# Rows of experts 1 to 7 gathered whole, sorted in DRAM and loaded again in the layout of the transposes; the last batch's routing in fewer steps

## The chip, the core and the metric

The kernel runs on one core of a Trainium2 chip. The metric is the device time of one execution in microseconds. TensorE (PE) does the products, VectorE (DVE) and ScalarE (ACT) the elementwise work, GpSimd (POOL) issues the gathers and scatters (indirect DMAs), and SyncE (SP) issues all other DMAs from one queue, in its program order.

## The reference

Attention over 4 batches, 8 heads, 768 positions and 64 columns a head, with 4 sink positions and a window of 128; then a mixture of 8 experts with two chosen for each of the 3072 tokens.

```python
x = attn_out.transpose(0, 2, 1, 3).reshape(B * S, H * D)          # 3072 x 512
noisy_logits = x @ w_gate + np.log1p(np.exp(x @ w_noise)) * noise
top2 = np.argpartition(-noisy_logits, 2, axis=1)[:, :2]
...                                                               # softmax over the two: top2_w
for e in range(E):
    for k in range(2):
        mask = top2[:, k] == e
        h = np.maximum(x[mask] @ w1[e], 0.0)                      # 512 -> 1024
        out[mask] += top2_w[mask, k, None] * (h @ w2[e])          # 1024 -> 512
```

## The kernel before

Phase one (to about 181 us) is the attention. It leaves each token's row in a DRAM array `x_rows`: 544 floats, in four quarters of 136 (`SW`: 128 columns of x and the 8 gate weights of the token). Phase two routes the last batch and runs the experts. Experts are sorted by their count of tokens; the first in that order is "expert 0" here, and capacities are 832 rows for the first four and 768 for the others, so an expert has 7 tiles of up to 128 rows or 6.

All work is recorded as operations of a planner, `Plan` (L80), each with an engine, a planned duration, a priority and the data that it reads and writes. Its `run` places them by a simulation of its own and writes a fixed program for every engine. So the order on each engine, and on SP's queue, is set by the planned durations, the priorities and the number of buffers; at run time an engine only waits for semaphores. `Plan.dma` records the issue on SP and the transfer.

**Expert 0** takes 4 tiles from batches 0 to 2 and 3 tiles (4 to 6) after the last batch is routed. Its rows are gathered whole (`go` in `gather`, L995, 128 rows of 544 floats), turned on PE (`rows_turn`, L1066), split into a high and a low half (ACT L1075, DVE L305), multiplied with w1 (`up`, L1285 to 1287), passed through ReLU (`up_h` on ACT, L1299; `up_l` on DVE, L1306) and multiplied with w2 (`down`, L1317 to 1323).

**Experts 1 to 7** form the first product by a scheme of seven half-size products (`seven`, L1420 to 1422). It needs x transposed, which DVE does in 32x32 blocks (`rows_seven`, L1194); for a tile to come out transposed in whole, each partition must hold four rows' quarters in a certain order. Therefore a tile is gathered in four pieces by quarters (`part`, L1001: 128 pieces of 136 floats), by an index table `rt_idq` with one entry for each quarter, which `spread` (PE L935, four groups of matmuls, DVE L938) builds at the end of the last batch's routing. There are 174 such gathers. They go into four buffers `xg`. After the transposes come the splits and sums of the scheme (DVE L305, ACT L1208). Weights are loaded by SP in pieces of 512 KB into two buffers `st` (`w_chunk`, L1102), and split by ACT (L1111, L1152) and DVE (L305, L1160). Before a tile's gathers stands a copy on POOL (`begun`, L1012) that holds them until the expert before has come to a certain point. The second product is L1451 and L1454; ends of a tile are ACT L1326 or ACT L1329 and DVE L1333, L1337, and the scatter that adds into the output is POOL L1341. The zeros of the output are written by SP (L1608).

**Routing of the last batch** runs while PE works on expert 0: logits (PE L710, DVE L721, L726), the top two (DVE L803, L807), the one-hot table `m` (L816), the ranks by matmuls with it (PE L824 to 830), one-hot tables of position and of tile (DVE L878 to 885), the place of each token in the experts' lists (PE L895), the order of the experts (`ordered`, DVE L955 to 967), the indices `idg` (L919) of expert 0's tiles 4 to 6, and `rt_idq`.

Of the kernel before, what the change touches and what calls it, by code (L numbers as in the profile page):

```python
# [9 lines left out]
F32 = mybir.dt.float32  # L10
# [65 lines left out]
PORT = 9  # L76
# [554 lines left out]
def routing_setup(nc, pool, tmp, cst, sh):  # L631
# [14 lines left out]
    iota("io", [128, 128], [[1, 128]], 0, 0)  # L646
    iota("io1", [128, E * TE], [[1, E * TE]], 1, 0)
# [48 lines left out]
def logits(nc, plan, cst, sh, b, jj, z):  # L696
# [4 lines left out]
    xa, li = plan.next("X"), b * (NT // 2) + jj  # L701
    last = b == sh.B - 1
    tk, mk = ("lt", li), ("lm", li)
# [3 lines left out]
    def proj():  # L707
        p = get("X", xa, [128, 4, 128], F32, "ps")
        for i, g in enumerate(pairs):
            nc.tensor.matmul(p[32 * i:32 * (i + 1), :2, :], c["wbd"][:, i].rearrange("p h a e -> p (h a e)"),  # L710
                             get("xtn", g, [128, sh.S])[:, jj * 256:(jj + 1) * 256], start=True, stop=True)

    def copy():
        nc.scalar.activation(get(*tk, [128, 2, 128], F32, "sb"), get("X", xa)[:, :2, :], AF.Copy)

    def turn():
        for i in range(2):
            nc.tensor.transpose(get("X", xa)[:, 2 + i, :], get(*tk)[:, i, :], c["idf"])

    def scale():  # L720
        nc.vector.tensor_tensor(get(*mk, [128, 2, H, 2 * E], F32, "sb"),  # L721
                                get("X", xa)[:, 2:, :].rearrange("p t (h e) -> p t h e", h=H),
# [7 lines left out]
    op("PE", .57, z, proj, r=[("xt", n) for n in ns] + [("rc", 0)], w=[("X", xa)], u=[("xtn", g) for g in pairs] + region)  # L730
    op("ACT", .27, z, copy, r=[("X", xa)], w=[tk], u=region)
    op("PE", .25, z, turn, r=[tk], w=[("X", xa)], u=region)
    op("DVE", .34, z, scale, r=[("X", xa)] + [("rin", n // 2) for n in ns], w=[mk], u=[("ri", b)] + region)
# [3 lines left out]
def routing(nc, plan, cst, sh, b, t0, nt, z, xbuf):  # L737
# [31 lines left out]
    def step(eng, dur, fn, r=(), w=(), u=(), kind=0):  # L769
        u = [*u, ("old", 0)] if last else u  # L770
        plan.op(eng, dur, z if last else plan.now + PR.get("rt", .5), fn, [t(x) if isinstance(x, str) else x for x in r],
                [t(x) if isinstance(x, str) else x for x in w], u, kind=kind)

    def dve(fn, r, w, dur=.07 + .001 * 8 * nt, u=(), kind=0):
        step("DVE", dur, fn, r, w, u, kind)
# [4 lines left out]
    side = "DVE" if last else "Pool"  # L780
    s_ = v if last else gp

    def aux(fn, r, w, cols=8):
        step(side, .07 + .001 * cols * nt if last else .15 + .0021 * cols * nt, fn, r, w, kind=PORT)
# [36 lines left out]
    def rank():  # L821
# [12 lines left out]
    aux(lambda: s_.tensor_tensor(rt("z")[:, 1], rt("mx")[:, :, 1], rt("mx")[:, :, 0], op=OP.subtract), ["mx"], ["z"], 1)  # L834
    act(lambda: nc.scalar.activation(rt("z")[:, 1], rt("z")[:, 1], AF.Exp), [], ["z"])
    aux(lambda: s_.tensor_scalar(rt("den", [128, nt]), rt("z")[:, 1], 1.0, 1e-9, op0=OP.add, op1=OP.add), ["z"], ["den"], 1)
    dve(lambda: v.reciprocal(rt("z")[:, 0], rt("den")), ["den"], ["z"], .1)
    aux(lambda: s_.tensor_tensor(rt("z")[:, 1], rt("z")[:, 1], rt("z")[:, 0], op=OP.mult), [], ["z"], 1)
    aux(lambda: s_.tensor_tensor(rt("wd", full), rt("oh"), rt("z")[:, :, :, None].to_broadcast(full), op=OP.mult),
        ["oh", "z"], ["wd"], 16)  # L840
    aux(lambda: s_.tensor_tensor(rt("w", ab_), rt("wd")[:, 0], rt("wd")[:, 1], op=OP.add), ["wd"], ["w"])
# [16 lines left out]
    if last:  # L858
# [4 lines left out]
        dve(lambda: v.tensor_scalar(rt("v0", n0), c["slot"][:, 0, sh.FA:], rt("cnt")[:, :1], None, op0=OP.is_lt), ["cnt"], ["v0"], .07)  # L863
        dve(lambda: v.tensor_scalar(rt("e0", n0), rt("v0"), -1.0, 1.0, op0=OP.mult, op1=OP.add), ["v0"], ["e0"], .07)
        dve(lambda: v.tensor_scalar(rt("e0"), rt("e0"), c["dum"], 128.0, op0=OP.mult, op1=OP.add), [], ["e0"], .07)
# [5 lines left out]
    dve(lambda: v.tensor_scalar(rt("pp", pair, I32), rt("g"), 127, None, op0=OP.bitwise_and), ["g"], ["pp"], .08)  # L871
    dve(lambda: v.tensor_scalar(rt("tq", pair, I32), rt("g"), 7, None, op0=OP.logical_shift_right), ["g"], ["tq"], .08)
    dve(lambda: v.tensor_scalar(rt("vl", pair), rt("r2"), float(sh.CAP), None, op0=OP.is_lt), ["r2"], ["vl"], .08)
    dve(lambda: v.scalar_tensor_tensor(rt("tv", pair), rt("tq"), 1.0, rt("vl"), op0=OP.add, op1=OP.mult), ["tq", "vl"],
        ["tv"], .08)
    wide = [128, nt, E * TE]
    for k in range(2):
# [8 lines left out]
            [], [f"tc{k}"], 56)  # L886
    if not last:
        yield 1
# [24 lines left out]
    if last:  # L913
# [17 lines left out]
        quarters = lambda: get("X", xs, [128, 4, E * TE], F32, "ps", [128, 4, 128])  # L931

        def spread():
# [3 lines left out]
        step("PE", .5, spread, [("y", -3), "idw"], [("X", xs)])  # L937
        dve(lambda: v.scalar_tensor_tensor(get("rt_idq", b, [128, 4, E * TE], I32)[:, :, rest], quarters()[:, :, rest], 4.0,  # L938
# [829 lines left out]
```

## Time and profile before

| | us |
|---|---|
| median of 3 runs (761.93 to 764.37) | 762.06 |
| the profiled execution, its own time | 758.4 |
| its span | 756.7 |
| PE busy in the span | 704.2 (93%) |
| DVE busy | 548.9 (73%) |
| POOL busy | 432.0 (57%) |
| ACT busy | 410.0 (54%) |

All durations below are of the profiled execution. Its span leaves 1.7 us of its time outside, and its time is 3.66 us under the median. A row of the waits names the engine and line that waited, what ended the wait, and the total, the count and the longest in microseconds; "issue" is time in which the engine waited for nothing that the profile shows, and "remote" a release whose source it doesn't place. In the rows of stretches, PEclk is the granted clock of TensorE as a share of full speed and DMA the mean busy share of the 16 DMA engines.

### The profile page before, as it was taken

The numbers are of one execution on the slowest core, as the hardware profiler recorded it, in microseconds if no ns is written. First come the engines' busy times: TensorE is split into PE (matmuls) and PEld (weight loads), VectorE is DVE, ScalarE is ACT, GpSimd is POOL, SyncE is SP. The second block draws the span as 40 slices with busy tenths as digits, with TensorE's granted clock in tenths as the row PEclk, the third lists the DMA queues.
The fourth block names the chain that finished last, engine by engine and source line by source line (L and its number), as shares of the span: only waits on it lengthen the run. The fifth ranks groups of instructions, "written<-read, shape, count | busy, mean of one in ns | idle before, by whom it ended". The sixth has DMA issues, their size and how long they took to land.

```text
span 756.7 us, 13528 instructions
## 1 busy us (share of the span) xinstructions
PE 704.2 (93%) x4737; PEld 588.2 (78%) x4737; DVE 548.9 (73%) x1289; ACT 410.0 (54%) x924; POOL 432.0 (57%) x560
## 2 busy tenths in 40 slices
PE   5999998998998959999999999998999999899995
PEld 3665766666776949888988998797899889889984
DVE  6799999985734777785887688576958868595720
ACT  3978788784113455555564656454645655455521
POOL 5668798793075735575557565666746556651022
PEclk9999999999999979999999999999999999999998
DMA  8656787556252581438235632744472383454233
GB/s 295 175 180 192 218 248 185 188 124 197 72 186 46 93 228 44 138 76 161 65 114 94 144 97 78 129 111 135 89 161 68 115 172 94 127 99 105 56 43 43
DMA packets 59048, 98.08 MB, mean 130 GB/s; under 512 B 19264, under 2 KB 32576, under 8 KB 58976
## 3 DMA queue, kind: packets, MB, share of 16 engines
q1 hardware_dynamic: 45616, 69.99, 30.2%
q0 software_dynamic: 13360, 27.19, 20.9%
q8 instruction: 38, 0.62, 0.4%
q14 instruction: 34, 0.28, 0.1%
HBM read 68.95 MB, written 28.20 MB: 128 GB/s over the span
## 4 chain that ended last, share of the span: by engine, by line
PE 61%; DVE 13%; ACT 8%; DMA 7%; issue 5%; POOL 4%; SPq 0%; another core or an unknown queue 0%; POOLq 0%; DVEq 0%; ACTq 0%
PE Y L1451 19%; PE H L1420 5%; PE H L1422 5%; PE H L1421 5%; DMA out<-tmp,idx 3%; PE X L1420 2%; PE X L1421 2%; PE X L1422 2%; PE S L401 2%; POOL xg L1001 2%; ACT strip L522 2%; DMA st<-in_w2c 1%; DMA xg<-x_rows,idg 1%; DVE cbuf L412 1%; PE P L464 1%
## 5 line engine op out<-in xcount | busy, mean ns | idle before, releaser
L1001 POOL DMA_INDIRECT xg<-x_rows,rt_idq x174 | 183.4, 1054 | 60.2 <-issue 44.5
L1451 PE MATMUL Y<-w2a,hb 128*128 128x512 f32 x504 | 128.1, 393 | 0.0
L1451 PE MATMUL Y<-w2b,hb 128*128 128x512 f32 x504 | 125.6, 393 | 0.0
L1451 PEld LDWEIGHTS Y<-w2b,hb 128*128 128x128 f32 x504 | 94.5, 188 | 20.1
L1341 POOL DMA_INDIRECT out<-tmp,idx x34 | 62.9, 1849 | 81.8 <-ACT tmp L1326 68.5
L1451 PEld LDWEIGHTS Y<-w2a,hb 128*128 128x128 f32 x504 | 94.4, 188 | 19.0
L1421 PE MATMUL H<-x,wr 128*128 128x384 f32 (+1 forms) x224 | 77.9, 348 | 1.0 <-DVE x L305 1.0
L1420 PE MATMUL H<-xe,wr 128*128 128x384 f32 (+1 forms) x168 | 59.1, 352 | 13.9 <-ACT xe L1208 7.8
L305 DVE TENSOR_TENSOR wr<-st,wr 128x512 fp32r<-128x512 f32 (+1 forms) x86 | 60.0, 697 | 9.6 <-ACT wr L1152 8.8
L1152 ACT ACTIVATE wr<-st 128x512 fp32r<-128x512 f32 x84 | 52.3, 625 | 20.1 <-DVE st L305 19.8
L305 POOL TENSOR_TENSOR cbuf<-cbuf,mn 128x528 f32<-128x528 f32 x48 | 52.6, 1098 | 12.4 <-DVE mn L422 8.7
L1422 PE MATMUL H<-xe,wr 128*128 128x384 f32 (+1 forms) x168 | 58.3, 347 | 0.0
L401 PE MATMUL S<-kq 64*64 64x196 f32 (+1 forms) x768 | 47.8, 352 | 7.9 <-DVE cbuf L412 4.8
L1326 ACT ACTIVATE tmp<-Y,wc 128x512 f32<-128x512 f32 x31 | 21.3, 688 | 49.7 <-PE Y L1451 27.5
L1420 PEld LDWEIGHTS H<-xe,wr 128*128 128x128 f32 x168 | 31.9, 190 | 19.6 <-ACT xe L1208 8.2
L1341 POOL DMA_INDIRECT out<-turned,idx x18 | 31.7, 1758 | 25.6 <-ACT turned L1326 19.2
L1435 ACT ACTIVATE tmp<-H 128x384 f32<-128x384 f32 (+1 forms) x56 | 28.0, 500 | 32.8 <-PE H L1422 26.4
L1421 PEld LDWEIGHTS H<-x,wr 128*128 128x128 f32 x224 | 42.5, 190 | 3.1 <-DVE x L305 1.6
L1012 POOL COPY spacer<-hb 1x1 f32<-1x1 f32 x28 | 6.4, 230 | 66.0 <-ACT hb L1441 41.4
L412 DVE COPY_PREDICATED cbuf<-le,S 128x256 f32<-128x256 uint8 x80 | 33.7, 441 | 11.4 <-ACT cbuf L405 11.0
L401 PEld LDWEIGHTS S<-kq 64*64 64x64 f32 x768 | 22.5, 138 | 23.8 <-DVE cbuf L412 12.4
L1420 PE MATMUL X<-x,wr 128*128 128x384 f32 (+1 forms) x112 | 38.8, 347 | 0.4 <-DVE tmp L1438 0.4
(329 smaller groups left out, 1804.1 us busy)
## 6 DMA issues: line engine op xcount, KB each, us to landing
st<-in_w1c SPq DMA_DIRECT2D x32, 512.0 KB
st<-in_w2c SPq DMA_DIRECT2D x32, 512.0 KB
kq<-in_qk_t SPq DMA_DIRECT2D x15, 780.0 KB
out<-zt SPq DMA_DIRECT2D x31, 256.0 KB
vn<-in_v SPq DMA_DIRECT2D x16, 384.0 KB
x_rows<-strip SPq DMA_DIRECT2D x48, 128.0 KB
xg<-x_rows,rt_idq POOLq DMA_INDIRECT x174
st<-in_vsink SPq DMA_DIRECT2D x4, 512.0 KB
```

Source lines behind the costliest of these rows:

```text
L305: eng.tensor_tensor(out, a, b, op=OP.subtract)
L401: nc.tensor.matmul(whole[x, h, c0:c1], kq(g)[r, KS + 128 * j + 64 * s:KS + 128 * j + 64 * s + 64], kq(g)[r, o + c0:o + c1], start=True, st ...
L412: nc.vector.copy_predicated(c, le[:, None, :].to_broadcast([128, 2, 128]), p)
L1001: nc.gpsimd.indirect_dma_start(out=x[:, i, :], out_offset=None, in_=xbuf.rearrange("r (q d) -> (r q) d", d=sh.SW), in_offset=bass.Indirect ...
L1152: plan.op("ACT", .03 + .255 * m, z, lambda: nc.scalar.activation(h(), src(), AF.Copy), r=[st], w=[(*key, b)] + old, u=[key, ex], lat=P2["s ...
L1326: nc.scalar.activation(get("y", Y[e, t], [128, DM]), get("Y", Y[e, t]), AF.Copy, scale=c["wc"][e % 2][:, t:t + 1])
L1341: d = nc.gpsimd.indirect_dma_start(out=out, out_offset=bass.IndirectOffsetOnAxis(ap=c["idx"][:size(e, t), e, t:t + 1], axis=0), in_=get("y ...
L1420: nc.tensor.matmul(p, wh, h, start=start and not k, stop=False, skip_group_check=True)
L1421: nc.tensor.matmul(p, wh, l, start=False, stop=False, skip_group_check=True)
L1422: nc.tensor.matmul(p, wl, h, start=False, stop=k == 1, skip_group_check=True)
L1435: nc.scalar.activation(u_of(e, k), src(), AF.Copy)
L1451: nc.tensor.matmul(p, h[:, x * (CAP + R) + 128 * t:x * (CAP + R) + 128 * t + 128], w[:, y], start=(f == 0 and x + y == 0), stop=(f == FC - ...
```

## The change

**Rows.** For experts 1 to 7 a tile's rows are gathered whole, by one indirect DMA of 128 rows of 544 floats instead of four by quarters (45 gathers instead of 174), into one of two staging buffers `sg`. SP stores the tile into a DRAM array `x_sorted`, by quarters, and loads it again into one of two buffers `xg` so that each partition holds four consecutive rows of one quarter, which is the layout for the transposes. Each of the 45 tiles so adds a store and a load of 278 KB (the last tile of a 832-row expert loads half) to SP's queue. Expert 0's tiles go to `sg` and `xg` too, by the table `row_tile`. The copies that hold gathers back are moved: expert 1 has none; expert 2 waits for points in expert 0's second part; experts 3 to 7 for points two experts earlier.

**Routing of the last batch.** The index table needs one matmul and one cast (`rt_idi`) instead of four groups of matmuls and one larger DVE operation. The odd piece of the logits gets a PSUM buffer of its own (`TX`). The one-hot tables are written by 24 tensor-scalar operations, one a tile, instead of six tensor-tensor operations; the gate weights' operations go from DVE to POOL; some operations that nothing waits for soon come later (`after=9`).

**Expert 0.** `up` is recorded as four operations instead of one. Two splits of weights (128x1024 each, one of w1 and one of w2) go from DVE to POOL, and the last piece of w2 is loaded later.

```diff
+def row_tile(sh, e, t):
+    n = sh.first[e] + t
+    if e:
+        return "xg", n - sh.first[1] + 2
+    return ("xg", t - 2) if t in (2, 3) else ("sg", t - 2 * (t > 3))
...
-    for i in range(min(128, sh.CAPS[e] - 128 * t) // 32):
-        plan.op("Pool", P2["gather"], z + i, lambda i=i: part(i), r=[("rt_idq", sh.B - 1)] + held,
-                w=[("xg", n, i)], u=[("xg", n)], lat=(P2["rest"], P2["lands"]))
+    def store():
+        nc.sync.dma_start(rows.rearrange("q p d -> p q d"), stage().rearrange("p (q d) -> p q d", d=sh.SW))
+
+    def load():
+        x = plan.get(*row, [128, sh.XW], F32, "early")[:, :size // 32 * sh.SW]
+        nc.sync.dma_start(x, rows.rearrange("q (s i) d -> (q s) (i d)", i=4)[:, :size // 32 * sh.SW])
...
+    plan.op("Pool", P2["gather"], zs, sort, r=[("rt_idi", sh.B - 1)] + held, w=[sg], lat=P2["lands"])
+    plan.dma(zs, store, 1.6, r=[sg], w=[("xs", n)], late=P2["late"])
+    plan.dma(z, load, 1.4, r=[("xs", n)], w=[row], late=2)
...
-            for q in range(4):
-                nc.tensor.matmul(quarters()[:, q, rest], get("y", -3, [128, 4, 128])[:, q, :], idw()[:, rest], start=True, stop=True)
+        step("PE", .15, lambda: nc.tensor.matmul(spread()[:, rest], get("y", -3, [128, 128]), idw()[:, rest], start=True, stop=True),
+             [("y", -3), "idw"], [("X", xs)])
...
+    for k in range(2) if last else ():
+        dve(lambda k=k: rows_of(k), ["pp"], [f"op{k}"], .1 * nt, kind=PORT)
+        dve(lambda k=k: cols_of(k), ["tv"], [f"tc{k}"], .085 * nt, kind=PORT)
...
-            w_chunk(plan, nc, c, sh, w1, w2, 0, 1, 3, -60)
-            for i in (2, 3):
-                w_chunk(plan, nc, c, sh, w1, w2, 0, 2, i, -50)
+            w_chunk(plan, nc, c, sh, w1, w2, 0, 1, 3, -60, "Pool")
+            w_chunk(plan, nc, c, sh, w1, w2, 0, 2, 2, -50, "Pool")
...
-        if t < XG and e == 1:
-            k = 5 * t // 3
+        if e == 1:
+            return None
+        if e == 2:
+            k = FC + t
             return ("hh", k), lambda: hs(k)[:1, :1].bitcast(F32), ("h", k)
-        if t < XG:
-            return ("h", e - 1, 2 * t, 0, 0), lambda: mine(plan)[:1, 2 * t, :1].bitcast(F32), ("hb", e - 1)
-        n, i = sh.first[e] + t - 1, 3
-        return ("xg", n, i), lambda: get("xg", n).rearrange("p (i d) -> p i d", d=sh.SW)[:1, i, :1], ("xg", n)
+        return ("h", e - 2, t, 0, 0), lambda: mine(plan)[:1, t, :1].bitcast(F32), ("hb", e - 2)
...
-            {"st": 2, "w1": 4, "w2a": 2, "xg": XG, "wc": 2, "xe": 1, "wr": 1, "x7": 1},
+            {"st": 2, "w1": 4, "w2a": 2, "xg": 2, "sg": 2, "wc": 2, "xe": 1, "wr": 1, "x7": 1},
```

POOL from expert 0's tiles 4 to 6 (`idg`) through the first gathers of expert 1 (`rt_idq`, now `rt_idi`) to the first scatters (L1341, now L1374). Before:

```order
L995 DMA xg<-x_rows,idg 128x544 x3
L1012 COPY spacer<-hb 1x1
L1001 DMA xg<-x_rows,rt_idq 128x136 x16
L1340 MEMSET spacer 1x1
L1341 DMA out<-turned,idx 3968x512
L1012 COPY spacer<-xg 1x1
L1340 MEMSET spacer 1x1
L1341 DMA out<-tmp,idx 3968x512
L1001 DMA xg<-x_rows,rt_idq 128x136 x4
```

After:

```order
L1015 DMA sg<-x_rows,idg 128x544 x3
L1030 DMA sg<-x_rows,rt_idi 128x544 x5
L1045 COPY spacer<-hb 1x1
L1373 MEMSET spacer 1x1
L1374 DMA out<-turned,idx 3968x512
L1030 DMA sg<-x_rows,rt_idi 128x544
L1045 COPY spacer<-hb 1x1
L1373 MEMSET spacer 1x1
L1374 DMA out<-tmp,idx 3968x512
L1373 MEMSET spacer 1x1
L1374 DMA out<-tmp,idx 3968x512
L1030 DMA sg<-x_rows,rt_idi 128x544
```

Sixteen gathers of quarters (four tiles) become five whole gathers (five tiles) ahead of the first scatter; expert 1's tile 5 stands behind that scatter, and its tile 6 behind the third of them as listed.

SP's queue over the same time, with the semaphores that a row waits for (DMASW is a gather or scatter that has landed, DMAHW a transfer of SP's own). Before, between the last loads of the experts' numbers and the next weight load:

```order
L1608 DMA out<-zt 128x512 [waits DMAHW3_49]
L1608 DMA out<-zt 128x512 [waits DMAHW4_49]
L1608 DMA out<-zt 128x512 [waits DMAHW5_49]
L1102 ISA
L1102 DMA st<-in_w2c 128x1024 [waits DMAHW1_49,DMAHW6_49,DVE_49,Activation_49]
L1608 DMA out<-zt 128x512 [waits DMASW7_49,DMASW6_49,DMAHW7_49,DMASW5_49,DMASW0_49]
```

After, the store and the load of expert 1's last tile, up to the next weight load:

```order
L1035 DMA x_sorted<-sg 128x4x136 [waits DMAHW2_49,DMASW0_49]
L1642 DMA out<-zt 128x512 [waits DMASW6_49,DMASW7_49,DMASW4_49,DMASW1_49]
L1642 DMA out<-zt 128x512 x3
L1035 DMA x_sorted<-sg 128x4x136 [waits DMASW2_49]
L1039 DMA xg<-x_sorted 128x272 [waits DMAHW2_49,DMAHW0_49,DVE_49]
L1642 DMA out<-zt 128x512 [waits DMAHW1_49]
L1642 DMA out<-zt 128x512
L1642 DMA out<-zt 128x512 [waits DMAHW3_49]
L1035 DMA x_sorted<-sg 128x4x136 [waits DMAHW4_49,DMASW3_49]
L1135 ISA
L1135 DMA st<-in_w2c 128x1024 [waits DMAHW5_49,DVE_49,Activation_49]
```

The load of expert 1's last tile (128x272) stands behind zeros that wait for four scatters and behind a store of expert 2; the weight load stands behind a further store.

DVE in the last batch's routing, the one-hot tables between the ranks and PE's matmuls of the places. Before:

```order
L878 TENSOR_TENSOR strip<-io,strip 128x768
L874 SCALAR_TENSOR_TENSOR strip<-strip 128x12
L878 TENSOR_TENSOR x_3050<-io,strip 128x768
L882 TENSOR_TENSOR strip<-io_85,strip 128x336
L882 TENSOR_TENSOR x_3050<-io_85,strip 128x336
L885 TENSOR_TENSOR strip<-strip,tok 128x336
L885 TENSOR_TENSOR x_3050<-x_3050,tok 128x336
```

After:

```order
L967 TENSOR_REDUCE tmp<-tmp 128x8
L873 TENSOR_SCALAR tmp<-tmp 128x12
L864 TENSOR_SCALAR tmp<-turned 128x3
L968 TENSOR_TENSOR perm<-io,tmp 128x64
L875 SCALAR_TENSOR_TENSOR tmp<-tmp 128x12
L877 SCALAR_TENSOR_TENSOR tmp<-tmp 128x12
L969 TENSOR_TENSOR tmp<-perm,turned 128x64
L882 TENSOR_SCALAR strip<-io,tmp 128x128 x6
L887 TENSOR_SCALAR strip<-io_85,tmp,tok 128x56 x6
L882 TENSOR_SCALAR x_3050<-io,tmp 128x128 x6
L887 TENSOR_SCALAR strip<-io_85,tmp,tok 128x56 x6
```

Six operations on whole tables become 24 on one tile's part each, and the start of the experts' order (L967 to L970) now stands ahead of them.

## Rows read from the trace of the kernel before

**Rows 1.** Waits of PE from 195 us on: us in total, times, longest us.

```profile
PE H L1420 <- ACT xe L1208: 7.8, 1, 7.8
PE H L1420 <- issue: 4.6, 3, 2.2
PE H L1420 <- ACT tmp L1435: 4.1, 4, 1.9
PE Y L1317 <- issue: 2.0, 2, 1.6
PE TX L1066 <- DMA xg<-x_rows,idg: 1.1, 1, 1.1
PE H L1421 <- DVE x L305: 1.0, 1, 1.0
```

**Rows 2.** Stretches: length; busy PE, PEld, DVE, ACT, POOL; PEclk, DMA share, GB/s.

```profile
232.00:236.00 4.00, 3.49 (x10) 2.57 (x10) 1.50 (x5) 0.98 (x2) 1.89 (x2) 0.57 0.07 17
240.00:260.00 20.00, 20.00 (x115) 18.21 (x114) 16.26 (x44) 10.40 (x22) 15.48 (x17) 1.00 0.53 74
267.60:275.30 7.70, 0.03 (x1) 0.03 (x1) 6.90 (x17) 4.68 (x10) 2.73 (x3) 0.63 0.88 283
275.30:280.00 4.70, 3.74 (x10) 3.18 (x11) 3.44 (x9) 1.79 (x5) 2.90 (x3) 0.51 0.76 89
280.00:520.00 240.00, 234.07 (x1127) 208.57 (x1126) 177.10 (x393) 126.44 (x250) 144.22 (x158) 1.00 0.46 106
648.40:652.00 3.60, 3.60 (x13) 3.60 (x12) 2.26 (x6) 1.99 (x4) 1.42 (x3) 0.53 0.52 125
```

**Rows 3.** The chain of work from 195 to 280 us: start, length, what.

```profile
212.11 3.71 DMA xg<-x_rows,idg
...
270.72 0.63 DVE turned L1194
...
274.36 0.43 DVE turned L1194
```

**Rows 4.** POOL's rows around expert 1's gathers: start, length, operation, idle before.

```profile
216.03 0.97 POOL L1001 DMA_INDIRECT xg<-x_rows,rt_idq  x1 [0.16 <-issue]
...
229.81 0.94 POOL L1001 DMA_INDIRECT xg<-x_rows,rt_idq  x1 [0.30 <-issue]
...
251.18 2.10 POOL L1341 DMA_INDIRECT out<-tmp,idx  x1 [0.23 <-ACT xe L1208]
...
264.32 0.95 POOL L1001 DMA_INDIRECT xg<-x_rows,rt_idq  x1 [0.31 <-issue]
```

**Rows 5.** ACT's row that waited for a late release of PE.

```profile
647.53 0.49 ACT L1435 ACTIVATE strip<-H 128x384 f32<-128x384 f32 x1 [4.46 <-remote]
```

**Rows 6.** The chain, PE's products of expert 0 and the last logits.

```profile
182.84 0.24 PE H L1287
...
191.88 0.57 PE X L710 x8
```

**Rows 7.** DVE's rows in the last batch's routing.

```profile
200.98 0.21 DVE L816 TENSOR_TENSOR m<-oh 128x48 bf16<-128x48 f32 x1
...
203.84 0.95 DVE L878 TENSOR_TENSOR strip<-io,strip 128x768 f16<-128x768 f32 x1
...
210.88 0.15 DVE L919 TENSOR_TENSOR idg<-x,tmp 128x3 int32<-128x3 f32 x1
...
214.52 0.36 DVE L938 SCALAR_TENSOR_TENSOR rt_idq<-X,quad 128x196 int32<-128x196 f32 x1 [2.17 <-PE X L935]
```

**Rows 8.** The chain, transfers that it waited for, issue to landing.

```profile
36.24 2.68 DMA vn<-in_v
...
153.58 3.83 DMA vn<-in_v
...
344.18 6.74 DMA st<-in_w2c
```

**Rows 9.** Waits of SP's queue from 195 to 300 us.

```profile
SPq L1102 <- DVE wr L305: 45.4, 1, 45.4
```

More of the change, by code (lines that the diff above doesn't have):

```diff
@@ L65 @@
 WIDE = 416
-XG = 4
-P2 = dict(rest=2.4, ga=-57.86, gs=4.26, wt=-28.03, x=-83.35, xs=13.55, wa=-27.67, ws=27.26, w2=-33.31, w2s=11.84, wb=1.97,
-          slack=0.55, sums=0.55, lands=5.78, late=0.93, gather=1.39, pair=5.89, a=1.92, b=7.67, d=7.57, c=-0.02,
+P2 = dict(sg=.01, ga=-57.86, gs=4.26, wt=-28.03, x=-83.35, xs=13.55, wa=-27.67, ws=27.26, w2=-33.31, w2s=11.84, wb=1.97,
+          slack=0.55, sums=0.55, lands=3.2, late=0.93, gather=1.27, pair=5.89, a=1.92, b=7.67, d=7.57, c=-0.02,
           e=-5.07, f=-4.27, g=3.49)
@@ L700, in logits @@
     c, get, op = cst, plan.get, plan.op
-    xa, li = plan.next("X"), b * (NT // 2) + jj
     last = b == sh.B - 1
+    tag = "TX" if last and jj % 2 else "X"
+    xa, li = plan.next(tag), b * (NT // 2) + jj
     tk, mk = ("lt", li), ("lm", li)
@@ L729, in logits @@
     region = [("old", 0)] if last else []
[L730 to L733, printed above, removed]
+    op("PE", .57, z, proj, r=[("xt", n) for n in ns] + [("rc", 0)], w=[(tag, xa)], u=[("xtn", g) for g in pairs] + region)
+    op("ACT", .27, z, copy, r=[(tag, xa)], w=[tk], u=region)
+    op("PE", .25, z, turn, r=[tk], w=[(tag, xa)], u=region)
+    op("DVE", .34, z, scale, r=[(tag, xa)] + [("rin", n // 2) for n in ns], w=[mk], u=[("ri", b)] + region)
     op("DVE", .5, z, total, r=[mk], w=[("lgs", li)], u=[("lg", b)] + region)
@@ L875, in routing, with rows_of, cols_of @@
         ["tv"], .08)
+    def rows_of(k):
+        o = rt(f"op{k}", [128, nt, 128], F16)
+        for i in range(nt):
+            v.tensor_scalar(o[:, i, :], c["io"], rt("pp")[:, k, i:i + 1], None, op0=OP.is_equal)
+    def cols_of(k):
+        o = rt(f"tc{k}", [128, nt, E * TE], F16)
+        for i in range(nt):
+            v.tensor_scalar(o[:, i, :], c["io1"], rt("tv")[:, k, i:i + 1], c["tok"][:, T0 + i:T0 + i + 1], op0=OP.is_equal, op1=OP.mult)
     wide = [128, nt, E * TE]
-    for k in range(2):
+    for k in range(2) if not last else ():
         dve(lambda k=k: v.tensor_tensor(rt(f"op{k}", [128, nt, 128], F16),
@@ L1057, in rows_turn @@
     s = slice(o, o + size)
-    n = sh.first[e] + t
+    row = row_tile(sh, e, t)
     ti = plan.next(ring)
@@ L1214, in rows_seven @@
     for t in group:
[L1215 to L1216 removed]
+        ni = min(128, sh.CAPS[e] - 128 * t) // 32
+        plan.op("DVE", .16 * ni, z, lambda t=t: blocks(t), r=[row_tile(sh, e, t)], w=[raw_], u=[("old", 1)], lat=(.06, P2["sums"]))
     split(0, 2, lambda: raw(0))
@@ L1282, in up @@
         w = w[:, :, :, f % 2 * 128:(f % 2 + 1) * 128]
-        for i in range(DC):
-            xh, xl = (x[:, i, :width] for x in both)
-            nc.tensor.matmul(p, w[:, 0, i], xh, start=(i == 0), stop=False)
-            nc.tensor.matmul(p, w[:, 0, i], xl, start=False, stop=False)
-            nc.tensor.matmul(p, w[:, 1, i], xh, start=False, stop=(i == DC - 1))
+        xh, xl = (x[:, i, :width] for x in both)
+        nc.tensor.matmul(p, w[:, 0, i], xh, start=(i == 0), stop=False)
+        nc.tensor.matmul(p, w[:, 0, i], xl, start=False, stop=False)
+        nc.tensor.matmul(p, w[:, 1, i], xh, start=False, stop=(i == DC - 1))
     def cut(q):
@@ L1390, in experts @@
                 zero(plan, nc, c, sh, out, i, zu, [("hh", k)])
+        if not q:
+            w_chunk(plan, nc, c, sh, w1, w2, 0, 2, 3, -50, first=[("hh", 2)])
         for a, t in enumerate(order):
```

141 lines of the change are left out of this document (74 added, 67 removed).

## The prediction

> **What bounds the kernel now.** I read the waits of PE first, since PE is busy in 234.07 of 240 us of a stretch of the later experts [rows 2]: a gain can only come from time in which PE stands still, or runs at half clock, or from less work of PE, and the change takes almost none of its work away. The waits [rows 1] show one large gap, 7.8 us ahead of expert 1's first product (L1420), ended by ACT's first split of its rows. Around it lie small ones: 1.1 us for a gathered tile of expert 0, 2.0 of "issue" in its second product, 1.0 between expert 1's first products. After that come 4.1 us, four times for `tmp` of ACT, and 4.6 us of "issue", three times. The stretches come next [rows 2]. In 267.6 to 275.3 PE does nothing and DVE is busy for 6.9 of 7.7 us; the granted clock falls in it to 0.63 on the mean, and is at 0.51, the lower level of 1.2 GHz, until 280, so 4.7 × 0.49 = 2.3 us of work are lost there. It was low too at 232 to 236 (0.57: 1.7 us) and at 648.4 to 652 (0.53: 1.7 us), each time after a gap of PE. Last the chain [rows 3]: expert 1 starts late because two of its tiles are transposed only at 270.72 and 274.36, and POOL issued the last of its quarter gathers at 264.32 [rows 4]. POOL takes 1.25 us for each (0.94 and 0.31 idle), and expert 1 needs 26, with scatters and waits between.
>
> PE could have begun expert 1 without its gaps at 275.3 − 7.8 − 1.1 − 2.0 − 1.7 = **262.7 us**.
>
> **Last batch's routing.** Between the first of the last logits and the ranks stood 72 products of expert 0 on PE; now 48 (24 × 0.24 us = 5.8 [rows 6]), because the odd logits have a buffer of their own and `up` is cut in four. The one-hot table `m` was ready at 200.98 [rows 7], right when PE reached the ranks, so both move: some 5.6 us earlier. The 24 tensor-scalar operations cost between 24 × 0.15 and 24 × 0.21 = 3.6 to 5.0 us [rows 7], and replace two of 0.95 and four of half that, 3.8: I take +0.5. Operations put off, or moved to POOL, save about 1 us in front of `idg`. So `idg` comes some 6 us before 210.88, at about 205. `rt_idq` at 214.52 had waited 2.17 us for PE's eight matmuls; one matmul and a cast between cut products bring it to about 207, 7.5 us earlier. None of this is on the path by itself; it only dates the gathers.
>
> **Expert 1's rows.** A whole gather took 3.71 us from start to landing [rows 3]. The trace shows no load or store between these arrays; the nearest are loads of 384 KB, 2.68 us in a quiet place and 3.83 in a busy one [rows 8]. For 278 KB I take 2.7 for the store and 2.7 for the load, at most 3.83 each, and no less than 1.9 (2.68 × 278 / 384). A tile's trip is 9.1 us (7.5 to 11.4), and a staging buffer is bound for 3.7 + 2.7 = 6.4. From 207 on, two buffers, first used by expert 0's tiles, bring five tiles in by about 236, just about when 16 quarter gathers were through before (229.81 is the twelfth [rows 4]). So the gain does not come from these five. It comes from the last two, which had ten more gathers of 1.25 us, and waits for one another, up to 264.32. Now they are one gather each, behind the first and the third of expert 0's scatters. The third was at 251.18 [rows 4]; with the gaps before it gone (1.1 + 2.0 + 1.7 = 4.8) it is at 246.4. The gather then starts at about 248.5, lands at 252.2, is stored by 254.9 and loaded by 257.6 (259.9 by the upper bound). In SP's queue this load stands behind zeros that wait for scatters; these have landed by then if a scatter takes no longer than a gather, 3.7 us. DVE then has to transpose and split, 0.9 us from the last transposition at 274.36 to the first product. DVE was busy for 16.26 of 20 us at 240 to 260 [rows 2], and it must do the same work for expert 1 in a shorter time; two splits of weights that go to POOL give some of it back. So the rows are ready between 259 and 265; PE is free at 262.7. I take the start at **264.0: −11.3 us**. The wait of 1.0 goes too, since it has the same cause, and without a gap of 7 us the clock does not fall: −2.3. Together **−14.6**.
>
> **Later experts.** On POOL 129 gathers less save 129 × 1.25 = 161 us of issue, which is not on the path. But PE's releases arrive late at places that fall in with long runs of quarter gathers: one of two such rows is ACT's wait of 4.46 us at 647.53 [rows 5], after twelve gathers on end, and PE's gap and the low clock at 648.4 follow it. Twelve on end stand at 216.03 to 229.81 too [rows 4], ahead of the low clock at 232. The trace does not say by what mechanism. In the new order the longest run is eight, and from the third on each waits for one of two staging buffers. At stake are 4.6 + 4.1 [rows 1] + 1.7 = 10.4 us; between nothing and all of it goes, and I take half: **−5.2**.
>
> **What is added.** 45 stores and 45 loads stand in SP's one queue among the 56 weight loads of experts 1 to 7. A store waits for its gather, a load for DVE's transposition of two tiles before, and whatever is behind them waits too. The queue has slack: SP stood 45.4 us on one wait for a weight buffer without PE being held [rows 9], and from expert 3 on the gathers are issued an expert ahead. The DMA engines were busy 0.46 in 280 to 520 [rows 2] while moving 106 GB/s; 25 MB more over 480 us are 52 GB/s, by proportion a share of 0.69. So there is room on the mean; I put **+1.0** for a new gap here and there, between 0 and what the rival below costs.
>
> **The sum.** −14.6 − 5.2 + 1.0 = −18.8 on the profiled 758.4: 739.6. The median stood 3.66 over that execution; with the same distance the forecast is **743.3 us**.
>
> **The rivals.**
> *SP's queue becomes the bound (slower).* A weight load now stands behind a row store that waits for its gather, which in turn waits for a point of an earlier expert. If in each of experts 2 to 7 a weight load, or the rows, come one gather too late (3.71 us), that is 6 × 3.71 = 22.3, against −14.6 and nothing from later experts: 758.4 + 7.7 + 3.7 = 769.8. It decides from 14.6 / 6 = 2.4 us an expert. For it: weight loads were on the chain already (6.74 us at 344.18 [rows 8]). Against it: the 45.4 us of slack, and stores that are issued an expert ahead. The Trainium skill ("DMA: Bandwidth & Descriptors", section "Issuing engines are not separate DMA queues") says that transfers run on the same 16 DMA engines whichever engine starts them and interleave there, so the added bytes would lengthen the weight loads and the gathers alike, and this rival would have nearer 0.15 than 0.11. The trace agrees with the rule in so far as the share is 0.88 where zeros, weights and gathers meet [rows 2].
> *Only expert 1 gains.* The late releases have another cause and stay: 743.3 + 5.2 = 748.5.
> *DVE is the bound ahead of expert 1.* Its work doesn't fit in the shorter time, or the last tile's load is late behind the zeros; expert 1 starts at 270 (−5.3), the clock falls all the same and the 1.0 stays: 758.4 − 5.3 − 5.2 + 1.0 + 3.7 = 752.6.
> *Everything goes.* Expert 1 starts at 262.7, all 10.4 us later vanish, no new gap: 743.3 − 1.3 − 5.2 − 1.0 = 735.8.
> *It does not do what it says.* The trip through DRAM takes as long as the quarter gathers did, 11.4 us a tile in pairs, expert 1 starts where it did and small new gaps eat the rest: 762.
>
> **How the numbers follow.** The forecast, 738 to 748 by its own bounds, has 0.47; only expert 1 gains 0.17; DVE the bound 0.12; everything goes 0.08; no difference 0.05; SP's queue 0.11. Leaving out the last two and a little below leaves 0.16 to 0.2 outside: the range is 734 to 757. A measurement of this kernel can tell about 0.3% (2.3 us) from no change; faster by more than that 0.84, within it 0.05, slower 0.11.
>
> **What would show it.** Right: expert 1's first product at 262 to 266 in the trace of after, no gap over 2 us ahead of it and a full clock behind it; `rt_idi` near 207; no releases of over 2 us called "remote" in later experts; POOL's last gather of expert 1 near 249. Wrong: a wait of PE for weights or for ACT's splits in experts 2 to 7 that repeats; SP waiting on a gather in front of a weight load that ACT then waits for; the first product of expert 1 after 270; or phase one, which should end at the same time, moved.

## The result, and the profile after

The changed kernel takes **739.33 us** in the median of 4 executions (737.07 to 740.64), the kernel before 761.99 (761.65 to 764.37): a ratio of 0.969 (95% interval 0.966 to 0.973). The forecast was 743.3, from 734 to 757. The profiled execution takes 739.88, 18.5 less than that of before.

Where it went, by the starts of PE's products in the two timelines (us):

| stretch | before | after | difference | forecast |
|---|---|---|---|---|
| start to the last batch's first logits | 181.5 | 183.1 | +1.6 | 0 |
| from there to expert 1's first product | 93.8 | 82.2 | −11.6 | −11.3 |
| expert 1 | 72.9 | 69.6 | −3.3 | −3.3 |
| experts 2 and 3 | 140.2 | 142.3 | +2.1 | |
| expert 4 | 67.7 | 62.8 | −4.9 | |
| expert 5 | 62.4 | 63.8 | +1.4 | |
| expert 6 | 67.5 | 62.7 | −4.8 | |
| expert 7 and the end | 70.6 | 71.8 | +1.2 | |
| span | 756.7 | 738.3 | −18.4 | |

For experts 2 to 7 the forecast was −5.2 and +1.0, together −4.2; it is −5.0. The engines' shares by the profile page of after (busy us, share of the span, instructions):

```profile
PE 700.4 (95%) x4731; PEld 587.1 (80%) x4731; DVE 546.5 (74%) x1300; ACT 409.1 (55%) x924; POOL 324.5 (44%) x431
```

PE does the same work in a shorter span. Its four longest waits from 195 us on (total, times, longest, in us), to be held against [rows 1]:

```profile
PE H L1455 <- ACT tmp L1470: 1.7, 1, 1.7
PE X L1455 <- ACT x L1241: 1.1, 1, 1.1
PE TX L1099 <- DMA sg<-x_rows,idg: 0.9, 1, 0.9
PE X L1456 <- DVE x L304: 0.8, 1, 0.8
```

The wait of 7.8 us ahead of expert 1 is gone, and so are all of "issue". The largest that are left belong to expert 2, at 337 to 352 us; the row on L1099 is expert 0's. Stretches, to be held against [rows 2] (length; busy PE, PEld, DVE, ACT, POOL; PEclk, DMA share, GB/s):

```profile
28.00:32.00 4.00, 4.00 (x48) 2.67 (x44) 3.23 (x6) 2.81 (x10) 2.12 (x4) 0.71 0.71 210
240.00:260.00 20.00, 20.00 (x111) 17.88 (x110) 16.73 (x47) 9.31 (x20) 10.32 (x17) 1.00 0.96 237
257.00:265.30 8.30, 8.30 (x45) 7.08 (x44) 7.66 (x23) 4.67 (x11) 1.40 (x4) 1.00 0.96 305
265.30:280.00 14.70, 14.42 (x74) 13.71 (x74) 13.36 (x33) 9.29 (x21) 9.38 (x11) 1.00 1.00 263
280.00:520.00 240.00, 236.33 (x1138) 210.88 (x1137) 181.89 (x404) 129.74 (x253) 85.35 (x91) 1.00 0.66 174
```

PE is busy right up to expert 1's first product at 265.30, and the clock stays whole behind it. DVE is busy in 7.66 of the 8.30 us ahead of it, so little room is left there. The DMA share of 280 to 520 rose from 0.46 to 0.66 at 174 GB/s; the proportion had given 0.69. The row of 28 to 32 us, with the clock at 0.71, is a dip in phase one that goes with 1.3 of the 1.6 us in the table's first row.

DVE's rows in the last batch's routing, the transposition of expert 1's last tile, and POOL's gather of that tile (start, length), to be held against [rows 3, 4, 7]:

```profile
206.67 0.14 DVE L935 TENSOR_TENSOR idg<-tmp 128x3 int32<-128x3 f32 x1
...
208.95 0.21 DVE L951 CAST rt_idi<-X 128x49 int32<-128x49 f32 x1 [0.39 <-PE X L948]
...
263.69 0.44 DVE L1227 STREAM_TRANSPOSE turned<-xg 128x256 f32<-128x256 f32 x1
...
245.40 1.25 POOL L1030 DMA_INDIRECT sg<-x_rows,rt_idi  x1 [0.30 <-issue]
```

`idg` comes 4.2 us earlier than before, the table of the rows 5.6 us, the last transposition 10.7 us. Expert 1's last gather is at 245.40, where before it was at 264.32.

### The profile page after: what moved, and what is told of

Read it like the earlier page. It is cut to its first block, busy times and chain, and to the rows that moved or that the text cites. A ratio compares the mean times of both kernels' runs of the same rounds, so it can differ in the third digit from the quotient of the medians.

```text
span 738.3 us, 13436 instructions
## 1 busy us (share of the span) xinstructions
PE 700.4 (95%) x4731; PEld 587.1 (80%) x4731; DVE 546.5 (74%) x1300; ACT 409.1 (55%) x924; POOL 324.5 (44%) x431
## 4 chain that ended last, share of the span: by engine, by line
PE 73%; DVE 9%; ACT 7%; DMA 6%; issue 2%; POOL 1%; SPq 0%; POOLq 0%; ACTq 0%; DVEq 0%
PE Y L1486 28%; PE H L1455 5%; PE H L1456 5%; PE H L1457 5%; PE X L1455 3%; PE X L1457 3%; PE X L1456 3%; PE S L400 2%; ACT strip L521 2%; DMA st<-in_w2c 2%; PE P L463 2%; DMA out<-tmp,idx 2%; PE Y L1489 2%; PE X L485 1%; PE H L1318 1%
## 5 line engine op out<-in xcount | busy, mean ns | idle before, releaser
L1374 POOL DMA_INDIRECT out<-tmp,idx x34 | 80.5, 2367 | 157.0 <-ACT tmp L1359 149.0
L1030 POOL DMA_INDIRECT sg<-x_rows,rt_idi x45 | 48.6, 1080 | 54.6 <-DMA x_sorted<-sg 32.1
L1455 PE MATMUL H<-xe,wr 128*128 128x384 f32 (+1 forms) x168 | 58.2, 347 | 2.5 <-ACT tmp L1470 1.7
L304 POOL TENSOR_TENSOR cbuf<-cbuf,mn 128x528 f32<-128x528 f32 x48 | 52.5, 1096 | 11.9 <-DVE mn L421 7.3
L1457 PE MATMUL H<-xe,wr 128*128 128x384 f32 (+1 forms) x168 | 57.6, 343 | 0.0
L1374 POOL DMA_INDIRECT out<-turned,idx x18 | 36.2, 2012 | 36.5 <-ACT turned L1359 30.2
L1045 POOL COPY spacer<-hb 1x1 f32<-1x1 f32 x38 | 12.0, 315 | 89.0 <-ACT hb L1476 81.8
L411 DVE COPY_PREDICATED cbuf<-le,S 128x256 f32<-128x256 uint8 x80 | 33.8, 442 | 12.1 <-ACT cbuf L404 11.7
L304 DVE TENSOR_TENSOR w2a<-st,w2a 128x1024 fp32r<-128x1024 f32 x16 | 19.6, 1223 | 27.3 <-ACT w2a L1144 27.3
```

The costliest lines, as they stand in the source:

```text
L304: eng.tensor_tensor(out, a, b, op=OP.subtract)
L411: nc.vector.copy_predicated(c, le[:, None, :].to_broadcast([128, 2, 128]), p)
L1030: nc.gpsimd.indirect_dma_start(out=stage(), out_offset=None, in_=xbuf, in_offset=bass.IndirectOffsetOnAxis(ap=cst["idw"]()[:, sh.TE * e + ...
L1374: d = nc.gpsimd.indirect_dma_start(out=out, out_offset=bass.IndirectOffsetOnAxis(ap=c["idx"][:size(e, t), e, t:t + 1], axis=0), in_=get("y ...
L1455: nc.tensor.matmul(p, wh, h, start=start and not k, stop=False, skip_group_check=True)
L1457: nc.tensor.matmul(p, wl, h, start=False, stop=k == 1, skip_group_check=True)
```

## The experiments

Times are medians; the ratio is to the kernel before on the same chip in the same session, with its 95% interval. The kernels ran on different chips, and the kernel before takes 749.5 us on one and 764 to 765 on another, while after takes 737.6 and 739.8 there. So only ratios and kernels of one chip are compared. By its time of before, 762, the result above is of a chip like the second.

| kernel | chip | us | ratio to before there | expert 1 starts |
|---|---|---|---|---|
| after, again | first | 737.6 | 0.984 (0.978 to 0.990) | 266.6 |
| routing only | first | 750.9 | 1.003 (0.999 to 1.006) | 269.1 |
| rows only | first | 741.9 | 0.992 (0.988 to 0.995) | 273.9 |
| before, paced | first | 753.8 | 1.007 (1.004 to 1.010) | 274.7 |
| before, again | second | 765.1 | (1.002: itself) | 280.4 |
| quarters staged | second | 777.2 | 1.021 (1.014 to 1.028) | 285.0 |
| store twice | second | 744.5 | 0.977 (0.971 to 0.984) | 269.9 |
| expert 2 sooner | second | 734.4 | 0.964 (0.958 to 0.971) | 264.5 |
| after, third | second | 739.8 | 0.969 (0.964 to 0.975) | 264.0 |
| expert 2 sooner, again | second | 735.6 | 0.963 (0.958 to 0.968) | 265.9 |
| no edits of expert 0 | second | 745.2 | 0.976 (0.971 to 0.981) | 274.1 |
| before, third | second | 764.8 | (0.999: itself) | 280.7 |

### The two halves of the change

**Routing only** is after with the gathers, buffers, index table, holding points and planned durations of before (`gather`, `begun`, `spread`, `rows_seven`, `P2`):

```diff
-    plan.op("Pool", P2["gather"], zs, sort, r=[("rt_idi", sh.B - 1)] + held, w=[sg], lat=P2["lands"])
-    plan.dma(zs, store, 1.6, r=[sg], w=[("xs", n)], late=P2["late"])
-    plan.dma(z, load, 1.4, r=[("xs", n)], w=[row], late=2)
+    for i in range(min(128, sh.CAPS[e] - 128 * t) // 32):
+        plan.op("Pool", P2["gather"], z + i, lambda i=i: part(i), r=[("rt_idq", sh.B - 1)] + held,
+                w=[("xg", n, i)], u=[("xg", n)], lat=(P2["rest"], P2["lands"]))
```

> The kernel before with the last batch's routing, the four-part up and the splits on POOL of after, and the rows of experts 1 to 7 still gathered by quarters. Theory (the rows do it): idg and the quarter table come some 5 us earlier, but expert 1's last two tiles still need ten quarter gathers behind scatters, so expert 1 starts at 270 to 274 us instead of 275.3, and the late releases in the later experts stay: 754 to 760 us. Rival (the routing does it): expert 1 starts at 265 to 267 and the time is 744 to 749 us.

**Rows only** is before with these lines the other way round.

> The kernel before with the rows of after (whole gathers, staging, the trip through DRAM, the new points that hold them), and the last batch's routing, the up in one piece and the splits on DVE as before. Theory (the rows do it): the last two tiles come early enough all the same; expert 1 starts at 267 to 270 us, the later experts gain about 8 us as in after: 742 to 748 us. Rival (the routing does it): expert 1 starts after 272 us, 750 to 756 us.

**After, again** ran beside them.

> The changed kernel itself, run again beside the others. Theory: the profiled execution lost 1.3 us in phase one to a low granted clock at 24 to 32 us, which is no part of the change (PE's order of phase one is the same in both kernels); an execution without it has an expert 1 that starts near 264.0 us. Expected median 737 to 741 us. Rival: the 1.3 us belong to the change (DMAs or other work that the change put into phase one) and show again at the same place.

The median of after, again is as expected, and the clock at 28 to 32 us is 1.00 in it, so the dip there does not come with the change. But its last logits start at 183.0 and expert 1 at 266.6 all the same, not near 264.0 as the theory had it.

The first chip's before took 749.5 us. Rows alone bring 7.6 us, the routing alone nothing (+1.4, its interval holds no change), both together 11.9. Rows only ends just under its theory's range, which was written for a chip of 762, while its expert 1 starts where the rival had it (273.9). The routing is not without effect: it moves the start of expert 1 to 269.1, between its theory and its rival and further than the rows do. Counted from the last batch's first logits, so that phase one drops out, expert 1 starts after 92.9 us in before, paced (below; the nearest there is to before on this chip), after 90.3 with the rows alone, 87.4 with the routing alone and 83.6 with both: 2.6, 5.5 and 9.3 us sooner. But the routing cannot keep the gain. The waits of PE in routing only:

```profile
PE H L1438 <- ACT xe L1225: 9.1, 3, 3.5
PE H L1439 <- DVE x L305: 2.8, 3, 1.2
```

There are three long waits for the first split, at the starts of experts 1, 2 and 3 (2.7, 2.9 and 3.5 us), where before has one [rows 1]; these experts last 75.2, 75.4 and 71.6 us, and in after, again 70.5, 72.8 and 68.9. The rows of experts 2 and 3 come late here too, and what expert 1 gains is given back behind it. Whether the quarter gathers make them late or the holding copies of before, at which POOL stands for 31.2 us between 270 and 425 us, this run does not tell: it has both. In rows only it is the other way round. The table of the rows, and the wait ahead of expert 1:

```profile
217.36 0.21 DVE L934 CAST rt_idi<-X 128x49 int32<-128x49 f32 x1 [1.55 <-PE X L931]
...
PE H L1437 <- ACT xe L1224: 6.0, 1, 6.0
```

The table is ready at 217.36, which is 2.8 us later than before [rows 7] (2.1 of it because the last logits start at 183.6 and not at 181.5), and PE stands still for 6.0 us. So a trip through DRAM by itself starts expert 1 hardly sooner than the quarter gathers did; it needs the early table. Why rows only still is 7.6 us below before on this chip is only half told: experts 2 to 6 last 68.8, 68.8 and three times 62.5 us, without any gap, but there is no trace of before on this chip to set against them.

### The edits of expert 0

After with `up` in one piece, the two splits back on DVE, and the last piece of w2 loaded in its old place:

```diff
-            w_chunk(plan, nc, c, sh, w1, w2, 0, 1, 3, -60, "Pool")
-            w_chunk(plan, nc, c, sh, w1, w2, 0, 2, 2, -50, "Pool")
+            w_chunk(plan, nc, c, sh, w1, w2, 0, 1, 3, -60)
+            for i in (2, 3):
+                w_chunk(plan, nc, c, sh, w1, w2, 0, 2, i, -50)
...
-            for i in range(DC):
-                op("PE", (UP1 * width + .19) / DC, zu, lambda q=q, f=f, i=i: up(q, f, i),
+            op("PE", UP1 * width + .19, zu, lambda q=q, f=f: up(q, f),
```

> The changed kernel without its edits of expert 0: the first product recorded as one operation again, and the two splits of weights back on DVE with the last piece of w2 loaded in its old place. The rows and the shortened routing stay. Theory (rows and routing date expert 1's rows, the edits of expert 0 give little): expert 1 starts at 265 to 268 us, 738 to 743 us. Rival (DVE has no room ahead of expert 1 without them, as the prediction's third rival has it): expert 1 starts at 269 us or later, 744 to 750 us.

The rival holds: 745.2 us, 5.5 above after on the same chip, and expert 1 starts at 274.1. PE's waits, and DVE's rows:

```profile
PE H L1454 <- ACT xe L1241: 6.0, 1, 6.0
PE TX L1099 <- DMA sg<-x_rows,idg: 2.6, 1, 2.6
...
213.36 0.15 DVE L935 TENSOR_TENSOR idg<-tmp 128x3 int32<-128x3 f32 x1
...
216.73 0.21 DVE L951 CAST rt_idi<-X 128x49 int32<-128x49 f32 x1 [1.95 <-PE H L1321]
...
272.15 1.21 DVE L304 TENSOR_TENSOR w2a<-st,w2a 128x1024 fp32r<-128x1024 f32 x1
273.28 0.43 DVE L1227 STREAM_TRANSPOSE turned<-xg 128x256 f32<-128x256 f32 x1
```

With `up` whole, the shortened routing is not short: `idg` comes at 213.36 and the table at 216.73, 8.0 and 9.1 us later than in after, third (below), on the same chip. The last tile is then transposed at 273.28, behind a split of weights of 1.21 us, and PE waits 6.0 us. The cut and the splits were not run apart, but PE's rows speak for the cut. The transposition of the first logits and the first product of the ranks, here:

```profile
187.86 0.38 PE L718 MATMUL X<-idf,turned 128*128 128x128 f32 x2
...
203.13 0.20 PE L824 MATMUL X<-m,tri 128*128 128x48 bf16 x1
```

and in after, third:

```profile
183.54 0.38 PE L718 MATMUL X<-idf,turned 128*128 128x128 f32 x2
...
195.93 0.20 PE L824 MATMUL X<-m,tri 128*128 128x48 bf16 x1 [0.38 <-DVE m L816]
```

The logits start at 182.39 here and at 181.74 there. With `up` whole the transposition stands behind twelve products of it (184.01 to 187.86, at a clock of 0.69 on the mean from 182.4 on), with `up` cut behind three; and the ranks follow `m` after 2.9 us (`m` at 200.26), behind twelve products again, where they follow it after 0.3. From the transposition to `m` the two take about the same, 12.4 and 12.1 us, although three splits of weights of 1.2 us stand on DVE between them here and none there. So the cut dates the table, and the splits hardly do.

### Late releases and the count of gathers

**Before, again** and **before, third** are the kernel before with a profile, to see it on the chip that it falls on.

> The kernel before itself, with a profile of the chip on which it took 749.5 us (22 executions, 744.4 to 752.9) and not 762. Theory (PE's late releases come and go with the chip or the execution, and cost about 12 us where they are): no wait called remote of over 2 us in this trace, experts 4 to 7 start 62 to 64 us apart where the first profile of before has 67.7 from expert 4 to 5 and 67.5 from expert 6 to 7, and expert 1 starts at 271 to 275 us; 745 to 753 us. Rival (the difference is spread, for example another clock or slower memory): the waits called remote are still there and all stretches are shorter by the same share.

> The kernel before with a profile on whichever chip this falls. Theory (with 174 quarter gathers PE's releases come late on some chips and not on others, and that is the 12 to 15 us between 749.5 and 764): where the time is near 750 there is no wait called remote of over 2 us and experts 4 to 7 start 62 to 64 us apart; where it is near 764, waits called remote of 2 to 8 us stand at 229 to 240 us and two of the experts last 66 to 69 us. Rival (the chips differ in clock or memory): the stretches differ by one share throughout.

Both fell on the second chip. The waits called remote of before, third:

```profile
ACT hb L1441 <- remote: 8.9, 2, 4.5
...
DVE tmp L1438 <- remote: 7.4, 2, 3.7
...
ACT hb L1299 <- remote: 6.8, 1, 6.8
```

As in the first profile [rows 5], experts 4 and 6 last long (68.6 and 65.3 us, expert 5 between them 62.4). **Before, paced** was to break the long runs of gathers by a wait for the tile ahead:

```diff
+        if t and e > 1:
+            n, i = sh.first[e] + t - 1, 3
+            return ("xg", n, i), lambda: get("xg", n).rearrange("p (i d) -> p i d", d=sh.SW)[:1, i, :1], ("xg", n)
```

> The kernel before, where from expert 2 on the quarter gathers of a tile are held by a copy that waits until the tile ahead has landed, so that no more than four quarter gathers stand on end (before: up to twelve). Theory (long runs of gathers make PE's releases late): the waits called remote of 3.8 us at 518 and 4.5 us at 647 and PE's gaps there vanish; 755 to 759 us. Rival (something else, such as the order of PE's work there): the gaps stay or move; 761 to 764 us.

It fell on the first chip and says nothing on its question: no wait called remote is in its trace, but none is in that of routing only either, which has the same 174 gathers in long runs and ran there too. It is 0.7% slower than before there; experts 5 and 6 last 65.1 and 63.7 us, and the last one with the end 76.0, with waits of PE for splits of rows (1.5 and 1.1 us in the last), so the pacing seems to make rows late. **Quarters staged** tells more. It is after, with four quarter gathers for each whole one into the same staging buffers, the rest as it is:

```diff
-    plan.op("Pool", P2["gather"], zs, sort, r=[("rt_idi", sh.B - 1)] + held, w=[sg], lat=P2["lands"])
-    plan.dma(zs, store, 1.6, r=[sg], w=[("xs", n)], late=P2["late"])
+    for i in range(4):
+        plan.op("Pool", P2["gather"], zs, lambda i=i: sort(i), r=[("rt_idi", sh.B - 1)] + held, w=[("sq", n, i)], u=[sg], lat=P2["lands"])
+    plan.dma(zs, store, 1.6, r=[("sq", n, i) for i in range(4)], w=[("xs", n)], u=[sg], late=P2["late"])
```

> The changed kernel, but each tile of experts 1 to 7 is gathered into its staging buffer by four quarter gathers instead of one whole (180 gathers instead of 45); the store, the load, the buffers and all the rest stay. It tells the count of gathers on POOL from the trip through DRAM and its two staging buffers. Theory of the prediction (fewer gathers bring expert 1's last two tiles in early): a tile costs 3 x 1.25 = 3.75 us more on POOL, in chains of two, expert 1 starts 7 to 10 us later and the time is 744 to 752 us. Rival (the waits for buffers and scatters set the gathers' times, not their count): 738 to 743 us.

It takes 777.2 us, 37 above after and 13 above before on that chip. A product, the row of ACT that reads it, and waits of PE:

```profile
231.40 0.39 PE L1325 MATMUL H<-xe,hb 128*128 128x512 f32 x1
...
240.18 0.93 ACT L1337 ACTIVATE hb<-H 128x512 fp32r<-128x512 f32 x2 [13.28 <-remote]
...
PE H L1460 <- ACT xe L1246: 11.7, 1, 11.7
PE H L1460 <- issue: 2.9, 4, 1.2
PE Y L1355 <- ACT hb L1337: 2.5, 1, 2.5
```

Expert 1 starts at 285.0 after a wait of 11.7 us, later than either theory had it, and the late releases are back. One wait of 13.3 us ends at 240 us, behind sixteen quarter gathers from 217.6 to 238.2; the product that this row reads had ended at 231.8, 8.4 us before. In before, third a row of ACT at 240.66 comes 10.1 us after the end of its product. On this chip both kernels with 174 and 180 gathers (before twice, quarters staged) show waits called remote in every profile; after, store twice, expert 2 sooner and no edits of expert 0, with 45 gathers, show none. So on that chip it is the gathering by quarters that brings them, not the layout or the trip; the count of gathers and the count of their pieces (four times as many, of 544 bytes) went together in every run and are not told apart. It is not shown why such gathers delay PE's releases, nor why the first chip, where routing only and before, paced have 174 (in paced sixteen on end), shows none; that before is 15 us faster there fits, but no trace of it was taken there.

### The price of the trip

**Store twice** writes each tile to a second array that nobody reads:

```diff
+    plan.dma(zs, store2, 1.6, r=[sg], w=[("xs2", n)], late=P2["late"])
```

> The changed kernel with each tile stored a second time into another DRAM array that nobody reads: 12.5 MB and 45 issues on SP more, and each staging buffer is free later. It prices the trip through DRAM. Theory (SP's queue and the DMA engines have room on the mean): 0 to 4 us more, 737 to 743 us. Rival (SP's queue is now near its bound, as the prediction's slower case has it): weight loads come late in each expert and the time is 750 us or more.

It costs 4.7 us against after on the same chip, a little over what the theory allowed and well short of the rival. The one long wait of PE that it adds is ahead of expert 1:

```profile
PE H L1459 <- ACT xe L1245: 5.8, 1, 5.8
```

Expert 1 starts at 269.9, 5.9 us later than in after, third, and lasts 2.5 longer; expert 2 gives 4.4 back, expert 3 loses 2.2, and experts 4 to 6 last 62.8, 62.8 and 63.6 us, much as in after. So the added stores find room on SP's queue and the DMA engines in experts 4 to 6; ahead of expert 1 there is none.

### Expert 2's rows

What after loses in expert 2 (73.4 us against 68.9 of expert 3) was put to the hold on its gathers:

```diff
         if e == 2:
-            k = FC + t
+            k = FC + t // 2
```

> The changed kernel, with expert 2's gathers held only by every second point of expert 0's second part, so that they may start sooner. Expert 2 takes 72.8 to 73.4 us in after where a like expert without gaps takes 68.8, and its waits for rows are 1.1 and 0.8 us. Theory (expert 2's rows are late because the two staging buffers and SP's queue are full with expert 1's, not because of the hold): no gain or a loss, 737 to 742 us. Rival (the hold makes them late): 733 to 737 us.

> The changed kernel with expert 2's gathers held only by every second point of expert 0's second part. Theory (from its first run: the hold made expert 2's rows late, and without it expert 2 takes 68.9 us): 3 to 6 us below the changed kernel on the same chip, 733 to 737 us. Rival (the first run was another chip's doing): within 1 us of the changed kernel.

**After, third** ran beside the second of them.

> The changed kernel once more, beside the version below that lets expert 2's gathers go sooner, on the same chip. Expected 736 to 741 us, expert 2 lasting 72 to 74 us with waits of PE for expert 2's splits at 337.

The waits of PE in after, third at expert 2, and those of expert 2 sooner, again over the whole:

```profile
PE X L1455 <- ACT x L1241: 1.5, 1, 1.5
PE X L1456 <- DVE x L304: 0.8, 1, 0.8
...
PE X L710 <- DVE xe L304: 1.4, 1, 1.4
PE X L1099 <- DVE xe L304: 0.6, 1, 0.6
PE TX L1099 <- DMA sg<-x_rows,idg: 0.4, 1, 0.4
```

My theory was wrong here: the hold did make expert 2's rows late. Without it expert 2 lasts 68.9 and 69.5 us instead of 73.2, no wait of PE in experts 1 to 7 is over 0.4 us (the last three rows above lie ahead of expert 1), and the time is 735.6 us beside 739.8, with executions of 734.26 to 736.88 and 738.44 to 741.59 that do not overlap. This version beats both kernels: 0.963 of before.

It also shows what the hold hides in the other runs. Where expert 1 starts late (rows only, no edits of expert 0, store twice), expert 2 lasts 68.8 us with the hold as well, which fits: its rows, held to points of expert 0, then have the time. So part of what such a run loses at expert 1's start comes back. In no edits of expert 0 a start 10.1 us later costs 5.5 us.

## Why the prediction was right, and where not

**What bounds the kernel: right.** The gain came out of PE's waits and its clock, and PE's busy time is nearly the same (704.2 and 700.4 us).

**Expert 1's start: the size right, the reason in part wrong.** The prediction had 264.0 us; the three profiles of after have 265.3, 266.6 and 264.0. The 2.3 us of clock and the wait of 1.0 went as worked out (expert 1: −3.3). But the prediction wrote of the routing that none of it is on the path by itself, and laid the gain on the last two tiles, one gather each instead of ten. The step that failed is this: from the last logits on, the routing alone brings expert 1's start 5.5 us forward, the rows alone 2.6, both 9.3; with the rows alone PE still waits 6.0 us, with the routing alone 2.7, and only with both it does not wait. What decides is the table that came 5.6 us earlier, and by the rows of no edits of expert 0 that hangs on the cut of `up`, which the prediction counted in its 24 products and then priced at nothing.

The trip through DRAM was mis-sized too. The prediction took 9.1 us for a tile and at most 11.4. The trip of expert 1's last tile in after, again, start and length of its gather and its store, and size and length of its load:

```profile
246.71 6.21 DMA sg<-x_rows,rt_idi
252.94 4.48 DMA x_sorted<-sg
...
xg<-x_sorted SPq DMA_DIRECT2D x1, 136.0 KB, 3.5
```

The load is issued at 257.67 and lands at 261.1, so the trip takes 14.4 us. In return the gather starts sooner than worked out, at 245.40 in the first profile against 248.5. That the start fits so well is in part luck.

**Routing: dates 2 us off.** `idg` was to come at about 205 and came at 206.67, the table at 207 and came at 208.95; 1.6 us of each is the later end of phase one.

**Later experts: mis-sized.** Half of 10.4 us was taken for the late releases. Experts 4 and 6, where they stood, gave 4.9 + 4.8 = 9.7, nearly all of it, on a chip that has them. The doubt that the prediction kept, whether gathers are the cause, is narrowed for that chip by quarters staged: it is the gathering by quarters. On the first chip, where no such release was seen, the change gives 11.9 us; there the rival by which only expert 1 gains (13.6 us) would have been the nearer one.

**What was added: mis-sized the other way.** +1.0 was taken; 2.1 (experts 2 and 3, of which expert 2 alone is +2.7), 1.4 and 1.2 us came, 4.7 in all. The two errors nearly cancel, by luck: −5.0 for experts 2 to 7 where −4.2 was forecast. The 2.7 come not from SP's queue in front of weights, as the slower rival had it, but from the hold on expert 2's gathers, which the prediction left without a price. The cause of the 1.4 and the 1.2 stays open: expert 5 lasts 62.9 to 63.8 us in the three profiles of after, the last expert 71.8 to 72.0. SP did come to wait on gathers with other issues behind it, 127.8 us in 36 times, and it cost PE nothing that can be seen:

```profile
SPq L1035 <- DMA sg<-x_rows,rt_idi: 127.8, 36, 9.2
```

**DVE ahead of expert 1.** The third rival did not decide in after, though by little: DVE is busy in 92% of the last 8 us, the last transposition ends 1.2 us ahead of the first product, and one more store a tile, or the splits and `up` as before, bring the wait of 6 us back.

**The basis: wrong by 4.** The sum on the profiled execution was 739.6 and came out at 739.88. The forecast added 3.66 us, the distance of before's median from its profile; that of after is −0.55. All of the 4.0 us between 743.3 and 739.33 is this step. The four profiles with waits called remote lie 1.6 to 5.7 us under the medians of their kernels, the ten without them between 1.3 us under and 3.1 over. So it fits that the distance of before is late releases, which differ in number and place from one profile to the next; it is not shown.

**Phase one** was to end at the same time and ended 1.6 us later in the first profile. It does not come with the change: the last batch's logits start at 181.5, 182.1 and 183.1 in the three profiles of before and at 183.1, 183.0 and 181.7 in those of after.

## What to carry to other kernels

When a stall has two chains that are about equally long, price each of them alone and both together before laying the gain on one: here each half gave little or gave it back later, and a small edit (cutting one block of PE work so that a short operation can pass) decided whether the other half counted. A hold that keeps transfers from starting too early is a price of its own; look who waits at the place that it serves. And where a profile shows waits without a source, try the kernel on another chip before their price goes into a sum.

## What the runs showed of the hardware

On one of two chips, waits whose source the profile doesn't place stand during or right behind runs of eight to sixteen quarter gathers that POOL issued 1.25 us apart. By what the waiting rows read they wait for PE: a row of ACT came 10.1 us after the end of its product (before, third) and one 8.4 us (quarters staged), and rows of DVE and POOL waited up to 3.7 and 3.0 us. Gaps of PE follow, and a granted clock of 0.53 to 0.58 behind them ([rows 2]; 0.58 at 240 to 244 us of quarters staged). With 45 whole gathers there is none. The kernel before differs by 15 us between the two chips, after by 2; before itself has no profile on the faster one.

A tile's trip of gather, store and load took 10.8 us for expert 1's first tile in after, again (218.05 to 228.82) and 14.4 for its last, where the DMA engines were busy 0.97 (240 to 260 us).

The Trainium skill ("DMA: Bandwidth & Descriptors", section "Issuing engines are not separate DMA queues") has it that all transfers share the 16 DMA engines, whichever engine starts them. The traces agree in so far as the share of these engines rose with SP's stores and loads, at 240 to 260 us from 0.53 to 0.96 and at 280 to 520 from 0.46 to 0.66. The 25 MB more did not make any weight load late enough to be seen in PE: no wait of PE in experts 4 to 7 of after is over 0.7 us.
